# Two barriers of a decode kernel: the first weight load issued ahead of the entry barrier, the closing barrier moved in among the last matmuls

## The chip, the cores and the metric

The profile lists the instructions of five engines. In the kernel before, TensorE (PE in the profile, PEld for its weight loads; 12682 of each) multiplies matrices, VectorE (DVE, 574), ScalarE (ACT, 454) and GpSimd (POOL, 27) do the other arithmetic, and SyncE (SP) issues the large loads, 280.50 MB on one queue, which 16 DMA engines carry out. The engines wait for each other by semaphores: in the program an instruction or a DMA raises a number (`then_inc`), and another engine waits until it has reached a value (`wait_ge`). A drain is an instruction that each engine has in front of a barrier. In the closing barrier of the kernel before, TensorE's ended 0.06 us behind its last matmul, VectorE's 0.05 us behind the copy, and SyncE's 0.48 us behind the issue of the store and 0.53 us ahead of the store's landing. A barrier is a place that no engine passes before all have reached it: in that one the last drain ended at 655.66 us and the first engine was released at 655.81. The granted clock is the share of its full clock that the profile shows for TensorE, 0.771 on average in the kernel before.

The kernel runs on one core of one Trainium2 chip. The metric is device time in microseconds (us), the lower the better. The kernel before took 657.67 us (median of 3 runs, 657.65 to 657.86), and 657.71 us over the 6 runs of the first comparison.

Two lengths occur in this text. The *time* is the metric. The *span* is what the profile draws: from the first recorded instruction to the last. The time is longer than the span by about 1.5 us. The result of each run lists its time to 0.01 us and its span to 0.1 us. Where "time minus span" is given below it is the mean over all runs of a kernel.

## The reference, cut to what matters

```python
def reference(A_x, A_k_cache, A_v_cache, A_wq, A_wo, B_x, B_w1, B_b1, B_w2, B_b2):
    # A: one decode token; 32 query heads, 8 KV heads, 65536 keys of 128, D = 512
    #    q = xn @ wq ; p = softmax(q k^T / sqrt(128)) ; o = p v ; result o @ wo
    # B: gelu(xn @ w1 + b1) @ w2 + b2, hidden size 1792
    x = A_x
    xn = _layernorm(x, axis=-1)
    return x + _A_ref(xn, A_k_cache, A_v_cache, A_wq, A_wo) + _B_ref(xn, B_w1, B_b1, B_w2, B_b2)
```

One token is decoded, so every weight and every cached key and value is read once. K and V are 134 MB each, wq and wo 4.2 MB each, w1 and w2 1.8 MB each. The output is 1 KB.

## The kernel before: the parts that matter

All large loads go out on SyncE's queue in a fixed order. Each wait is a semaphore wait that the program inserts from the recorded dependences.

```python
    dma_small()        # ACT queue: x row (1 KB), b2 (1 KB), b1 (3.5 KB)
    dma_wq()           # SP queue: 4 MB, no wait in front of it
    dma_w12()          # SP queue: w1, w2, 1.8 MB each
    issue_chunks()     # SP queue: K halves of 4 MB, V of 8 MB, as their slots come free;
                       # ... last of all wo in pieces (4, 2 and 1 KV heads, then 3+1 query heads)
```

The end, after the rolled loop over 16 pairs of K/V chunks:

```python
    for i, (g0, n) in enumerate(WP):                 # wo pieces 0, 1, 2
        for r in range(g0 * HPG, (g0 + n) * HPG):
            for kt in range(KT):
                fin_mm(kt, oX_bf[:, r:r + 1], wo_sb[:, r, ...], ["oX", f"wo{i}"], ...)
    for h in range(HPG):                             # the last piece: the last KV head's rows
        for kt in range(KT):
            fin_mm(kt, oT_all[:, ...], wl_sb[:, h, ...], ["oL", ...], ...)
    # copy PSUM -> fin_bf on DVE, store fin_bf -> out on SP
    # ...
    with nc.Block() as block:          # entering: jump of every engine into its own code
        # ... one body per engine: _emit(...) of everything recorded above
    # leaving the block: a barrier of all five engines
    sp.wait_ge(ev_out.sem, ev_out.val) # SyncE alone waits for the store
```

The barriers are not written out in the kernel. An entry barrier stands at the head of the program, behind the setting of some constants on GpSimd. A closing barrier stands where the block ends. In both, every engine drains and signals GpSimd, and GpSimd then releases all of them: in the entry barrier of the trace the last drain, GpSimd's, ends at 0.50 us, GpSimd's two semaphore instructions stand at 0.54 and 0.62, and the others are released at 0.66 to 0.67; in the closing barrier of the trace the last drain ends at 655.66 us, GpSimd's two semaphore instructions stand at 655.69 and 655.77, and the others are released at 655.81 to 655.82.

## Time and profile before

| | before |
|---|---|
| time, median of 3 | 657.67 us |
| span of the profiled execution | 656.2 us |
| moved | 280.65 MB, mean 428 GB/s |
| TensorE busy | 536.5 us (82%) |

The page's slice table cuts the span into 40 equal slices. A digit is the busy share in tenths, 9 meaning 90% or more. The DMA section names the queues.

```profile
span 656.2 us, 27968 instructions
...
PE   2387799978789697878969788896978879787897
...
DMA  8999999999999999999999999999999999999997
...
q1 hardware_dynamic: 8616, 280.50, 99.3%
```

The DMA engines are full from the second slice to the second last, while TensorE has gaps. The packet records in the trace say it more sharply: between 2.07 us and 651.63 us no stretch of over 150 ns has fewer than 12 of the 16 DMA engines at work. So the span is a first wait, then a stream that the DMA engines set and not the compute engines, then a tail.

The head, from the timeline (start, duration, engine, line, operation; `SPq` and `ACTq` are the queue instructions of SyncE and ScalarE; in brackets the idle time before and what ended it):

```profile
0.74 0.53 ACTq L454 DMA_DIRECT2D rows_bf<-in_A_x_dram  x1
...
0.75 0.39 SPq L463 DMA_DIRECT2D kv<-in_A_wq_dram  x1
...
1.20 0.41 SPq L467 DMA_DIRECT2D kv<-in_B_w_dram  x1
...
2.95 0.40 DVE L499 CAST x_row<-rows_bf 1x512 f32<-1x512 bf16 x1
...
8.75 0.16 DVE L521 CAST xnT_bf<-pA 128x4 bf16<-128x4 f32 x1 [0.38 <-PE pA L518]
...
13.30 3.15 PE L525 MATMUL pss<-kv,xnT_bf 128*1 128x512 bf16 x28 [4.59 <-DMA kv<-in_A_wq_dram]
```

SyncE drains at 0.00 us and is released at 0.66. The first packet of wq moves at 1.77 us, by the packet records. Layernorm is done at 8.9 us and TensorE then waits 4.59 us for wq.

The tail, from the timeline, and the instructions of the closing barrier (durations in ns, then the start in us):

```profile
652.62 0.39 PE L805 MATMUL pss<-kv,oX_bf 128*1 128x128 bf16 x16 [0.22 <-DMA kv<-in_A_wo_dram]
...
653.72 0.46 PE L805 MATMUL pss<-kv,oT_all 128*1 128x128 bf16 x16 [0.70 <-DMA kv<-in_A_wo_dram]
654.23 0.29 DVE L820 CAST fin_bf<-pss 97x128 bf16<-97x128 f32 x1 [5.01 <-PE pss L805]
654.55 0.63 SPq L824 DMA_DIRECT2D out_dram<-fin_bf  x1
```

```profile
L828 POOLq EVENT_SEMAPHORE  x2: 17/17/17, 655.7 to 655.8; - x2
...
L828 SPq DRAIN  x1: 417/417/417, 655.2 to 655.2; - x1
...
L828 PEldq EVENT_SEMAPHORE  x1: 51/51/51, 655.8 to 655.8; - x1
```

The queue's own waits of SyncE (us in total, times, longest):

```profile
SPq L850 <- DMA out_dram<-fin_bf: 0.4, 1, 0.4
SPq L828 <- PEq L828: 0.2, 1, 0.2
```

SyncE issues the store, drains for 0.42 us, passes the barrier at 655.8 us, and then still waits 0.4 us for the store.

### The profile page before, as it was taken

Reading aid. Unit: us, or ns where it says so; the run is one execution under the profiler, and the core shown is the slowest. Engines: PE = TensorE matmul, PEld = TensorE weight load, DVE = VectorE, ACT = ScalarE, POOL = GpSimd, SP = SyncE. Lnnn points to the kernel's source line nnn. Section 1 sums busy time; section 2 is a strip of 40 time slices with the busy share of each in tenths; the row PEclk is TensorE's granted clock in tenths of the full one; section 3 lists DMA queues with packets and bytes.
Section 4 is the critical chain, followed back from the end, with each engine's and each line's share of the span. In section 5 each row is a group of like instructions: output and inputs, shape, how many; then the busy total and the mean of one; then the engine's idle time right before and its main releaser. Section 6 shows DMA issues by size and latency. Waiting matters only on the chain.

```text
span 656.2 us, 27968 instructions
## 1 busy us (share of the span) xinstructions
PE 536.5 (82%) x12682; PEld 509.5 (78%) x12682; DVE 275.3 (42%) x574; ACT 244.9 (37%) x454; POOL 2.9 (0%) x27
## 2 busy tenths in 40 slices
PE   2387799978789697878969788896978879787897
PEld 0186798978688697868959787895978879786886
DVE  3244162725435162453516345261534516154353
ACT  0134162624425153352505335160443516244251
POOL 0000000000000000000000000000000000000000
PEclk9788596968869597786958778595876959688696
DMA  8999999999999999999999999999999999999997
GB/s 367 431 450 424 426 431 431 437 425 465 397 437 443 423 439 425 437 429 439 437 419 447 417 441 421 429 463 399 451 417 457 425 419 437 425 465 397 434 429 307
DMA packets 8774, 280.65 MB, mean 428 GB/s; under 512 B 1082, under 2 KB 1596, under 8 KB 1724
## 3 DMA queue, kind: packets, MB, share of 16 engines
q1 hardware_dynamic: 8616, 280.50, 99.3%
q8 instruction: 8, 0.13, 0.1%
q10 hardware_dynamic: 148, 0.01, 0.0%
q14 instruction: 2, 0.02, 0.0%
HBM read 280.50 MB, written 0.00 MB: 427 GB/s over the span
## 4 chain that ended last, share of the span: by engine, by line
DMA 64%; PE 34%; issue 2%; DVE 0%; SPq 0%
DMA kv<-in_A_k_cache_dram 61%; PE pst L590 27%; PE pss L610 4%; DMA kv<-in_A_wo_dram 3%; PE pO L681 2%; PE pA L637 0%; PE pA L648 0%; DVE pmax L618 0%; PE pA L697 0%; DVE gmax L639 0%; PE pss L805 0%; DVE diag L641 0%; SPq L470 0%; SPq L467 0%; SPq L463 0%
## 5 line engine op out<-in xcount | busy, mean ns | idle before, releaser
L600 ACT ACTIVATE kt_ring<-pst 128x1024 bf16<-128x1024 bf16 x192 | 195.6, 1027 | 310.7 <-PE pst L590 309.2
L590 PE MATMUL pst<-ident_bf,kv 128*128 128x128 bf16 x4096 | 282.0, 235 | 35.3 <-DMA kv<-in_A_k_cache_dram 35.2
L590 PEld LDWEIGHTS pst<-ident_bf,kv 128*128 128x128 bf16 x4096 | 263.7, 106 | 43.6 <-DMA kv<-in_A_k_cache_dram 36.8
L598 DVE COPY kt_ring<-pst 128x1024 bf16<-128x1024 bf16 x320 | 210.5, 687 | 120.4 <-PE pst L590 118.1
L681 PE MATMUL pO<-P_bf,kv 128*128 128x4 bf16 x4096 | 115.1, 166 | 38.2 <-DMA kv<-in_A_v_cache_dram 34.2
L681 PEld LDWEIGHTS pO<-P_bf,kv 128*128 128x128 bf16 x4096 | 113.6, 104 | 39.6 <-DMA kv<-in_A_v_cache_dram 35.3
L610 PE MATMUL pss<-q_cur,kt_ring 128*128 128x4 bf16 x4096 | 111.9, 164 | 4.3 <-issue 4.3
L610 PEld LDWEIGHTS pss<-q_cur,kt_ring 128*128 128x128 bf16 x4096 | 109.3, 96 | 4.5 <-issue 4.5
L659 ACT ACTIVATE P_bf<-pss,negm 128x128 bf16<-128x128 f32 x128 | 50.8, 547 | 68.0 <-DVE negm L651 68.0
L690 DVE COPY o_all<-pO 128x4 f32 (+1 forms) x32 | 5.2, 162 | 121.4 <-PE pO L681 120.6
L618 DVE TENSOR_REDUCE pmax<-pss 128x4 f32<-128x512 f32 x32 | 22.1, 691 | 68.2 <-PE pss L610 68.2
L659 ACT ACTIVATION_READ_ACCUMULATOR P_bf<-pss,negm 128x1 f32 x128 | 35.3, 276 | 0.0
L648 PEld LDWEIGHTS pA<-diag,ones_f 4*128 4x128 f32 x64 | 12.6, 244 | 17.9 <-DVE diag L641 16.3
L637 PE MATMUL pA<-ident_f,pmax 128*4 128x128 f32 x64 | 14.0, 307 | 12.5 <-DVE pmax L618 12.5
L648 PE MATMUL pA<-diag,ones_f 4*128 4x4 f32 x64 | 15.4, 309 | 10.0 <-DVE diag L641 10.0
L637 PEld LDWEIGHTS pA<-ident_f,pmax 128*4 128x4 f32 x64 | 2.9, 84 | 15.7 <-DVE pmax L618 14.0
L639 DVE TENSOR_REDUCE gmax<-pA 4x1 f32<-4x128 f32 x32 | 8.8, 274 | 9.2 <-PE pA L637 9.2
L673 DVE COPY sums_all<-sums 128x8 f32 (+1 forms) x16 | 2.7, 171 | 23.4 <-ACT P_bf L659 23.4
L697 PE MATMUL pA<-sums_all,ones_f 128*128 128x128 f32 x32 | 12.4, 491 | 0.0
L651 DVE TENSOR_SCALAR negm<-pA 128x4 f32<-128x4 f32 x32 | 5.1, 160 | 10.8 <-PE pA L648 10.8
L697 PEld LDWEIGHTS pA<-sums_all,ones_f 128*128 128x128 f32 x32 | 8.0, 312 | 0.0
L641 DVE TENSOR_SCALAR diag<-ident_f,gmax 4x4 f32<-4x4 f32 x32 | 6.9, 217 | 1.1
(78 smaller groups left out, 48.3 us busy)
## 6 DMA issues: line engine op xcount, KB each, us to landing
kv<-in_A_k_cache_dram SPq DMA_DIRECT2D x32, 4096.0 KB, 27.6
kv<-in_A_v_cache_dram SPq DMA_DIRECT2D x4, 4096.0 KB, 24.4
kv<-in_A_wq_dram SPq DMA_DIRECT2D x1, 4096.0 KB, 12.4
kv<-in_B_w_dram SPq DMA_DIRECT2D x2, 1792.0 KB, 18.2
kv<-in_A_wo_dram SPq DMA_DIRECT2D x1, 2048.0 KB, 24.2
kv<-in_A_wo_dram SPq DMA_DIRECT2D x1, 1024.0 KB, 26.4
kv<-in_A_wo_dram SPq DMA_DIRECT2D x1, 512.0 KB, 27.2
kv<-in_A_wo_dram SPq DMA_DIRECT2D x1, 384.0 KB, 17.6
```

The costliest lines, as they stand in the source:

```text
L590: lambda tb=tb, at=at, b=b, tt=s * TPB + t: pe.transpose(pst[tb][:, at * 128:(at + 1) * 128], slot[b][:, tt, :], ident_bf[:, :]),
L598: e, fn = DVE, lambda tb=tb, dst=dst: dve.tensor_copy(out=dst, in_=pst[tb][:, :])
L600: e, fn = ACT, lambda tb=tb, dst=dst: act.activation(out=dst, in_=pst[tb][:, :], func=ACTF.Copy)
L610: lambda k=k, kb=kb, at=at, t=t: pe.matmul(pss[k][:, at:at + HPG], lhsT=kt_ring[:, kb * BCOL + t * 128:kb * BCOL + (t + 1) * 128], rhs=q_c ...
L618: lambda k=k: dve.tensor_reduce(out=pmax[:, :], in_=pss[k][:, 0:CW].rearrange("p (t j) -> p j t", j=HPG), axis=AX.X, op=ALU.max),
L637: sch.op(PE, lambda: pe.matmul(pA[0:HPG, PA_ST:PA_ST + 128], lhsT=pmax[:, 0:HPG], rhs=ident_f[:, :], start=True, stop=True), reads=["pmax" ...
L639: sch.op(DVE, lambda: dve.tensor_reduce(out=gmax4[:, :], in_=pA[0:HPG, PA_ST:PA_ST + 128], axis=AX.X, op=ALU.max), reads=["pA"], writes=[" ...
L641: sch.op(DVE, lambda: dve.tensor_scalar(out=diag4[:, :], in0=ident_f[0:HPG, 0:HPG], scalar1=gmax4[0:HPG, 0:1], scalar2=None, op0=ALU.mult) ...
L648: sch.op(PE, lambda: pe.matmul(pA[:, PA_SB:PA_SB + HPG], lhsT=ones_f[0:HPG, 0:128], rhs=diag4[0:HPG, 0:HPG], start=True, stop=True), reads ...
L659: lambda k=k, at=at, j=j, src=src: act.activation(out=P_v[k][:, :, j], in_=src[:, :, j], func=ACTF.Exp, bias=negm[:, at:at + 1], scale=1.0 ...
L681: lambda k=k, t=t: pe.matmul(pO[:, 0:HPG], lhsT=vslot[:, k * TPD + t, :], rhs=P_v[k][:, t, :], start=t == 0, stop=t == TPD - 1),
L697: sch.op(PE, lambda: pe.matmul(pA[:, PA_SUM:PA_SUM + NC], lhsT=ones_f[:, :], rhs=sums_all[:, :], start=True, stop=True), reads=["ones_f", ...
```

## The change

The intent is to take both barriers off the ends. The load of wq waits for nothing, so it can be issued before SyncE reaches the entry barrier. The closing barrier can stand where TensorE would wait for the next wo piece anyway (0.54 us in the kernel before), and the last matmuls, the copy and the store then follow it.

```diff
+    rest = {}
     for i, (g0, n) in enumerate(WP):
+        if i == 1:
+            rest.update((e, len(e.ops)) for e in (PE, DVE, SP))
         for r in range(g0 * HPG, (g0 + n) * HPG):
@@
+    first, SP.ops[0] = SP.ops[0], ([], None, None)
+    assert not first[0]
+    head = nc.cur_bb.bb.instructions
+    n = len(head)
+    first[1]().then_inc(*first[2])
+    at = next(k for k, ins in enumerate(head) if ins.engine == mybir.EngineType.SP
+              and type(ins).__name__ == "InstDrain")
+    moved = [head.pop() for _ in range(len(head) - n)]
+    for ins in moved:
+        head.insert(at, ins)
@@
-            _emit(e, SP.ops)
+            _emit(e, SP.ops[:rest[SP]])
@@  (DVE and PE likewise)
+    for e, obj in ((PE, pe), (DVE, dve), (SP, sp)):
+        _emit(obj, e.ops[rest[e]:])
     sp.wait_ge(ev_out.sem, ev_out.val)
```

More of the change, by code (lines that the diff above doesn't have):

```diff
@@ L843, in _ @@
         def _(e):
-            _emit_rolled(e, DVE.ops, [m[0] for m in marks2], pair)
+            _emit_rolled(e, DVE.ops[:rest[DVE]], [m[0] for m in marks2], pair)
         @block.tensor
         def _(e):
-            _emit_rolled(e, PE.ops, marks)
+            _emit_rolled(e, PE.ops[:rest[PE]], marks)
+    for e, obj in ((PE, pe), (DVE, dve), (SP, sp)):
+        _emit(obj, e.ops[rest[e]:])
     sp.wait_ge(ev_out.sem, ev_out.val)
```

## The prediction

> What bounds the kernel now. The slice table shows the 16 DMA engines busy 0.9 or more in every slice but the first (8) and the last (7), at about 430 GB/s; the DMA section shows 280.5 MB on SyncE's queue. The transfer records are stricter: from 2.07 us to 651.63 us no stretch over 150 ns has fewer than 12 of the 16 engines at work. A 4 MB K transfer lands a median 27.6 us after its issue, though 4 MB at 430 GB/s takes under 10 us, so another transfer is always queued. TensorE is busy 82% but waits for K and V landings (35.2 and 34.2 us in the waits view). The span is therefore: time to the first byte, about 650 us of stream, and a tail after the last wo byte. This edit can change only the first and last.
>
> Head. In the timeline SyncE's drain stands at 0.00 us, the entry barrier releases it at 0.66, its wq issue runs 0.75 to 1.13, first data moves at 1.77. Issued ahead of the drain, wq should start at 0.0 to 0.1 and its first byte move at 1.0 to 1.1. Cost: SyncE reaches the barrier after its 0.39 us issue and a drain that may take as long as the one behind the store (0.42 us), so the barrier releases near 0.9 to 1.1. That delays the x row, the memsets and the layernorm by 0.2 to 0.4 us, which is free: layernorm was done at 8.9 us and TensorE then waited for wq until 13.3. The w1 issue stays near 1.0 to 1.2 us, while wq feeds the engines for about 10 us. The whole gain, 0.65 to 0.75 us, lies on the critical path, and as the queue never runs dry it should reach the end undiminished.
>
> Tail. The last wo piece lets TensorE go at 653.72; matmuls 0.49, copy 0.29, store issue 654.55 to 655.18, SyncE's drain 0.42, barrier released at 655.81, then still 0.4 us of wait until the store lands at 656.19. The closing barrier is already hidden behind the store's flight; moving it saves nothing.
> The moved barrier costs TensorE a drain (0.29 us) and a release (about 0.2 us) after the first wo piece, which ended at 650.83; the second started at 651.37. It may now start up to 0.2 us late, but pieces two and three wait 0.5 to 0.7 us for data afterwards, which absorbs it. Net tail: 0.
>
> Sum: 657.67 - 0.7 = 656.95; 0.1% faster, so "same". Range 656.6 to 657.4.
>
> What the profile would show. Right: first wq data near 1.05 us; stream length unchanged within 0.2 us; later landings 0.7 us earlier; the stretch from last matmuls to end still about 2.5 us and ended by the store's landing. Wrong: a slow first issue; a starved queue after wq; TensorE idle after the moved barrier for a reason other than data.
>
> What would make it wrong. [...] this trace has four waits of about 2 us in TensorE's first loop pass with no recorded cause. If the jump behind the barrier caused one, the gain becomes a loss of about 1 us. Or the measured time includes work after the last instruction that idle engines can start sooner: then up to 0.4 us more gain. Or the stream's rate differs by 0.1%, which hides everything.

## The result, and the profile after

The changed kernel took 656.82 us (median of 6 runs, 656.69 to 656.90) against 657.71 us for the kernel before. The ratio is 0.9986, with a 95% interval from 0.9973 to 0.9999. By the 2% rule that is "same". A ratio is the mean time of one kernel's fast runs over that of the other's in the same rounds, so it is not quite the ratio of the two medians.

The head after the change:

```profile
0.00 0.39 SPq L463 DMA_DIRECT2D kv<-in_A_wq_dram  x1
...
0.79 0.52 ACTq L454 DMA_DIRECT2D rows_bf<-in_A_x_dram  x1
...
0.80 0.33 SPq L467 DMA_DIRECT2D kv<-in_B_w_dram  x1
...
7.21 0.41 DVE L499 CAST x_row<-rows_bf 1x512 f32<-1x512 bf16 x1 [4.13 <-DMA rows_bf<-in_A_x_dram]
...
13.03 0.16 DVE L521 CAST xnT_bf<-pA 128x4 bf16<-128x4 f32 x1 [0.39 <-PE pA L518]
...
13.25 3.58 PE L525 MATMUL pss<-kv,xnT_bf 128*1 128x512 bf16 x32 [0.25 <-DVE xnT_bf L521]
```

The issue of wq now stands at 0.00 us and its first packet moves at 1.02 us. The barrier released SyncE at 0.71 us, only 0.05 us later than before: the drain behind this issue took 0.12 us and ended at 0.57, and in the kernel before the barrier had waited for GpSimd anyway, whose drain behind its constants ended at 0.50. But look at the x row. It is issued 0.05 us later and is used 4.3 us later, at 7.21. Its 1 KB packet moved at 5.53 us instead of 1.66 us: it now finds the DMA engines already full of wq (from 1.35 us on, 12 or more of the 16 at work). Its landing was told at 7.12 us instead of 2.00. The delay is more than one recorded packet of wq: those (32 KB each) took 1.2 to 2.2 us, and the x row moved 3.9 us later than before. How the DMA engines share their time between the two queues no run here shows. wq landed at 12.31 us instead of 13.17, but TensorE's first projection starts at 13.25 us instead of 13.30: it now waits for the layernorm, not for wq, and is no earlier than before.

The tail after the change:

```profile
650.55 1.02 PE L805 MATMUL pss<-kv,oX_bf 128*1 128x128 bf16 x32 [0.33 <-PEq L842]
...
651.76 0.60 PE L805 MATMUL pss<-kv,oX_bf 128*1 128x128 bf16 x16 [0.18 <-DMA kv<-in_A_wo_dram]
...
652.85 0.60 PE L805 MATMUL pss<-kv,oT_all 128*1 128x128 bf16 x16 [0.50 <-DMA kv<-in_A_wo_dram]
653.50 0.29 DVE L823 CAST fin_bf<-pss 97x128 bf16<-97x128 f32 x1 [4.78 <-PE pss L805]
653.82 0.64 SPq L827 DMA_DIRECT2D out_dram<-fin_bf  x1
```

```profile
L842 POOLq EVENT_SEMAPHORE  x2: 17/17/17, 650.3 to 650.4; - x2
...
L842 PEldq DRAIN  x1: 893/893/893, 649.4 to 649.4; - x1
...
L842 PEldq EVENT_SEMAPHORE  x1: 51/51/51, 650.4 to 650.4; - x1
```

```profile
SPq L866 <- DMA out_dram<-fin_bf: 1.0, 1, 1.0
```

```profile
SPq L866 <- DMA out_dram<-fin_bf: 1.0, 1, 1.0
```

The barrier releases TensorE at 650.44 us, and the second wo piece landed at that very moment, 650.44. The next two pieces again wait for data. SyncE waits 1.0 us for the store instead of 0.4, so the 0.6 us that the barrier took there became waiting: nothing was won inside the span.

Here is the whole difference of the two profiled executions, from the instruction, packet and landing records (us):

| stretch | before | after | difference |
|---|---|---|---|
| start to the first packet of wq | 1.77 | 1.02 | -0.75 |
| first packet to the end of the last wo packet | 651.72 | 651.61 | -0.11 |
| to the start of the last piece | 0.23 | 0.22 | -0.01 |
| last piece, up to the copy | 0.51 | 0.65 | +0.14 |
| copy to the end of the span | 1.99 | 1.99 | 0.00 |
| span | 656.22 | 655.49 | -0.73 |
| time minus span | 1.58 | 1.32 | -0.26 |
| time | 657.80 | 656.81 | -0.99 |

The time minus span is that of two single executions here; the means over all runs, below, differ by 0.17 us.

The +0.14 us goes with the granted clock. The two windows below (length, busy us and count of TensorE, granted clock, DMA share, GB/s) are of the same microsecond, before and then after:

```profile
653.00:654.00 1.00, 0.29 (x20) 1.00 0.05 17
```

```profile
653.00:654.00 1.00, 0.45 (x16) 0.50 0.00 0
```

The clock records alternate between 1.00 and 0.50 from 17.5 us to the end in the kernel before, in stretches of up to 20.5 us. Which of the two the last piece meets differs between the profiled executions (one of each program) and is not an effect of the change: in three of the later experiments that contain the whole change (e5, e6 and e7) the clock stands at 1.00 there and this stretch takes 0.51 us, in e1, e8 and e10 it stands at 0.50 and takes 0.65 us. For example e7:

```profile
653.00:654.00 1.00, 0.38 (x16) 1.00 0.00 0
```

Two things were left to explain. Is the head alone responsible for the shorter span? And where does the gain outside the span come from?

### The profile page after: what moved, and what is told of

Same layout as the page of the kernel before. It is cut to its first block, busy times and chain, and to the rows that moved or that the text cites. A ratio compares the mean times of both kernels' runs of the same rounds, so it can differ in the third digit from the quotient of the medians.

```text
span 655.5 us, 27968 instructions
## 1 busy us (share of the span) xinstructions
PE 536.8 (82%) x12682; PEld 509.6 (78%) x12682; DVE 275.8 (42%) x574; ACT 245.0 (37%) x454; POOL 2.9 (0%) x27
## 4 chain that ended last, share of the span: by engine, by line
DMA 63%; PE 34%; issue 2%; DVE 0%; SPq 0%
DMA kv<-in_A_k_cache_dram 61%; PE pst L590 27%; PE pss L610 4%; DMA kv<-in_A_wo_dram 3%; PE pO L681 2%; PE pA L637 0%; PE pA L648 0%; DVE pmax L618 0%; PE pA L697 0%; PE pss L805 0%; DVE gmax L639 0%; DVE diag L641 0%; SPq L470 0%; SPq L467 0%; DVE fin_bf L823 0%
```

## The experiments

The theory going in: the head earns the first byte's 0.75 us and the moved barrier earns nothing inside the span. For the 0.2 us outside the span there were two candidates. Theory A says it is noise, or tied to the shape of the code. Theory B says the time includes end work of each engine after its last recorded instruction, and idle engines start it sooner once the barrier is gone from the end. The rival is that the barrier was on the path inside the span.

All times below are means of the runs of one job (e1 to e4, e5 to e8, e9 to e11 and e12 each on one chip, with the kernel before beside them). All outputs are right.

| run | edit | time | against before of the job | span | time minus span |
|---|---|---|---|---|---|
| before (four jobs) | | 657.61 to 657.73 | | 656.14 to 656.23 | 1.46 to 1.51 |
| e1 | the whole change | 656.75 | -0.98 | 655.42 | 1.33 |
| e2 | head only | 656.98 | -0.74 | 655.48 | 1.50 |
| e3 | tail only | 657.52 | -0.20 | 656.16 | 1.36 |
| e4 | before, second closing barrier | 657.96 | +0.24 | 656.14 | 1.82 |
| e5 | change, GpSimd waits for the store | 657.40 | -0.32 | 655.52 | 1.87 |
| e6 | change, ScalarE waits | 657.03 | -0.69 | 655.52 | 1.50 |
| e7 | change, TensorE waits | 657.16 | -0.56 | 655.52 | 1.63 |
| e8 | change, VectorE waits | 657.05 | -0.66 | 655.58 | 1.48 |
| e9 | before, four more entry barriers | 659.27 | +1.55 | 657.52 | 1.74 |
| e10 | change, five loads ahead | 656.75 | -0.97 | 655.38 | 1.37 |
| e11 | change, barrier in front of the copy | 657.11 | -0.61 | 655.67 | 1.44 |
| e12 | tail only, four more entry barriers | 659.14 | +1.53 | 657.58 | 1.56 |

The intervals of the ratios are about 0.13 to 0.17% of the time wide on each side, near 1 us, so a single ratio proves little here: e3's -0.20 us has the interval 0.9984 to 1.0011. What carries the argument are the spans, the time minus span, and the records of the trace, which repeat much better (before: 1.50, 1.49, 1.51 and 1.46 us in four jobs).

### e1 to e3: the whole change and its halves

> The changed kernel again, as the yardstick for the parts on the same chip. Theory (the head alone pays inside the span): 0.85 to 0.95 us under before, span 0.7 us shorter, first wq data near 1.02 us instead of 1.77, the closing stretch ended by the store's landing. If the last pieces ran at granted clock 0.50 only by chance of phase, this profile may show 1.00 there, and then a span near 655.35.

e2 keeps the head part of the diff alone, e3 the tail part alone:

```diff
 # e2, against before
+    first, SP.ops[0] = SP.ops[0], ([], None, None)
+    ...                                     # the moved issue, as in the change
 # e3, against the change
-    first, SP.ops[0] = SP.ops[0], ([], None, None)
-    ...
```

> Only the first issue is moved. Theory A (closing barrier hidden behind the store, and nothing outside the span counts): all of the gain, 0.7 to 0.9 us, as e1_both within 0.1 us. Theory B (the time also holds work after the last instruction that the other engines start sooner once the barrier is gone from the end): the span shrinks by about 0.7 us but the time gains only about 0.7, some 0.2 us less than e1_both, and time minus span stays near 1.55 us as in before.

> Only the barrier is moved. Theory A: no change in span or time (within 0.15 us; the last piece may take 0.49 or 0.62 us by the granted clock). Theory B: span unchanged, time 0.2 us lower, time minus span near 1.33 us as in the changed kernel. Rival (the barrier was on the path): span 0.3 to 0.6 us shorter.

The head alone shortens the span by 0.74 us (656.22 to 655.48) and the time by the same 0.74 us. Its first packet moves at 1.02 us. The tail alone leaves the span where it was (656.22 and 656.16; its runs scatter from 655.9 to 656.5) and lowers the time minus span from 1.50 to 1.36 us. The halves add up: 0.74 + 0.20 is 0.94, against 0.98 for the whole. So the span's gain is the head's, and the gain outside the span is the moved barrier's. Noise, the one half of theory A, and the rival (an effect inside the span) both fall. Theory B fits, but these three runs do not exclude that the shape of the code sets the time outside the span; e4 to e8 take that up. e1's hope for a full clock at the end did not come true: the clock stood at 0.50 again.

### e4: a second barrier at the end

```diff
+    nc.all_engine_barrier()
     sp.wait_ge(ev_out.sem, ev_out.val)
```

> The kernel before with one more barrier right behind the closing one. The closing barrier releases at 655.82 us and the store lands at 656.19, so 0.37 us of slack. Theory A: a second barrier of about 0.2 to 0.3 us fits into the slack, span and time unchanged within 0.1 us. Theory B: span unchanged, time 0.2 to 0.3 us higher, because the other engines end that much later. Rival (barrier on the path): both 0.2 to 0.3 us higher.

The second barrier released the engines at 656.15 us instead of 655.82, and SyncE's wait for the store still ended the span: 656.2 us in the profile, a mean of 656.14. The time minus span went up from 1.50 to 1.82 us, by 0.32 us, as much as the release came later (0.33 us). So a cost can be entirely hidden within the span and still be paid in the time.

### e5 to e8: which engine?

Each of these is the changed kernel with one more line, for one engine each:

```diff
     sp.wait_ge(ev_out.sem, ev_out.val)
+    pool.wait_ge(ev_out.sem, ev_out.val)      # e5; act in e6, pe in e7, dve in e8
```

> The changed kernel, with GpSimd also waiting for the store at the very end. So far time minus span is 1.50 us where all engines are held by the closing barrier until 0.4 us before the end (before, head only), 1.82 with a second barrier, and 1.33 to 1.36 where the others were released 4 us earlier. Theory B: some engine has about 0.55 us more end work than SyncE. If it is GpSimd: span unchanged, time minus span about 1.9 us, time about 657.3. If not: 1.33 and 656.75. Theory A (outside-span time is noise or tied to the code's shape): no difference between the four engines.

> The same with ScalarE waiting for the store. If ScalarE has the longer end work: time minus span about 1.9 us, time about 657.3; if not 1.33 and 656.75.

> The same with TensorE waiting for the store. If TensorE has the longer end work: time minus span about 1.9 us, time about 657.3; if not 1.33 and 656.75.

> The same with VectorE waiting for the store. If VectorE has the longer end work: time minus span about 1.9 us, time about 657.3; if not 1.33 and 656.75.

The four engines now end at the same moment as SyncE, one at a time. The time minus span is 1.87 us for GpSimd, 1.63 for TensorE, 1.50 for ScalarE and 1.48 for VectorE, against 1.33 when SyncE ends alone. It is GpSimd, as one of the two outcomes had it; that the other three cost 0.15 to 0.3 us too had not been expected. These four programs differ in one engine's name alone, so the shape of the code does not explain their differences; what one more waiting instruction costs by itself none of them tells. Now the kernel before can be estimated: its GpSimd ended at 655.78 us, and 1.87 us more gives 657.65, while SyncE ended at 656.22 and 1.33 us more gives 657.55. By this estimate GpSimd, released by the closing barrier, was the engine that finished last in the kernel before, by about 0.1 us, a little less than the 0.14 to 0.18 us that the moved barrier gained. The same sum fits e4: GpSimd's last instruction ended at 656.12 us there, and 1.87 more gives 657.99, against a mean time of 657.96. In that time the traces of the kernel before and of the changed kernel list no instruction, but their semaphore records go on: 245 semaphores are updated once each between 0.31 and 0.98 us behind the span in the kernel before, and 234 between 0.26 and 0.85 us in the changed kernel. Which engine does it, and what else is done in that time, no run here shows.

### e9: the first byte delayed on purpose

```diff
+    for _ in range(4):
+        nc.all_engine_barrier()
     with nc.Block() as block:
```

> The kernel before with four more entry barriers, to dose the delay of the first byte. One barrier took 0.33 us in e4, so wq is issued at about 2.1 us and its first data move at about 3.1 us instead of 1.77. Theory (the head counts one to one, as the stream never runs dry): span and time both 1.3 us longer, about 659.0. Rival (the first loop passes or the layernorm set the pace, the stream catches up): clearly less than 1.3 us.

The issue of wq stood at 2.09 us and its first packet moved at 3.11 us instead of 1.77, 1.34 us later. The span grew by 1.31 us (656.21 to 657.52). The head counts one to one, in both directions. The time grew by more, 1.55 us, because the time minus span also grew, from 1.51 to 1.74 us. The account did not explain that, and e12 takes it up.

### e10: more loads ahead of the barrier

```diff
-    first[1]().then_inc(*first[2])
+    for _, fn, pub in SP.ops[:5]:
+        fn().then_inc(*pub)
+    SP.ops[:5] = [([], None, None)] * 5
```

> The changed kernel with all five first loads (wq, w1, w2, two K) issued ahead of the entry barrier, not wq alone. The entry barrier then releases near 2.5 us and the x row comes about 1.8 us later. Theory (only the first byte counts): first data at 1.02 us as before, time as the changed kernel within 0.15 us, 656.75; layernorm ends near 10.5 us, still before wq lands at 12.3. Rival (more issues ahead pay too): a further 0.2 us or more.

Nothing more was gained: a mean of 656.75 us, as e1. Only the first byte counts, because the queue behind it is never empty: by the packet records of e10 no stretch of over 150 ns has fewer than 12 DMA engines at work between 1.24 and 651.95 us, and in the changed kernel none between 1.35 and 651.52 us. One number of the expectation missed: layernorm was not done near 10.5 us. The x row was issued at 2.83 us, and the timeline of e10 shows what followed:

```profile
8.30 0.41 DVE L499 CAST x_row<-rows_bf 1x512 f32<-1x512 bf16 x1 [3.17 <-DMA rows_bf<-in_A_x_dram]
...
14.13 0.16 DVE L521 CAST xnT_bf<-pA 128x4 bf16<-128x4 f32 x1 [0.39 <-PE pA L518]
...
14.35 3.58 PE L525 MATMUL pss<-kv,xnT_bf 128*1 128x512 bf16 x32 [0.25 <-DVE xnT_bf L521]
```

The projection started 1.1 us later than in the changed kernel, 1.95 us after wq had landed at 12.40, and even that cost nothing. The first load that waits for this early work, a V load, was issued at 26.76 us in e10 instead of 25.00, while K loads issued before it landed until 41.56 us.

### e11: the barrier where nothing hides it

```diff
-        if i == 1:
-            rest.update((e, len(e.ops)) for e in (PE, DVE, SP))
@@
     NR = 32 * (KT - 1) + 1
+    rest.update((e, len(e.ops)) for e in (PE, DVE, SP))      # barrier behind the last piece
```

> The changed kernel with the barrier moved on, from the second wo piece to behind the last piece, in front of the copy and the store: there nothing hides it. Theory: TensorE's drain (0.29 to 0.43 us) and the release (about 0.15 us) stand between the last matmul and the copy, so the span grows by 0.3 to 0.5 us against the changed kernel, time minus span falls or stays at 1.33, time 657.05 to 657.25. Rival (a barrier is free wherever it stands as long as it is not last): 656.75.

In the profile of e11 the copy waits for the barrier:

```profile
652.77 0.59 PE L805 MATMUL pss<-kv,oT_all 128*1 128x128 bf16 x16 [0.46 <-DMA kv<-in_A_wo_dram]
653.70 0.29 DVE L822 CAST fin_bf<-pss 97x128 bf16<-97x128 f32 x1 [4.91 <-PEq L841]
```

From the start of the last piece to the copy it took 0.92 us, against 0.65 in the changed kernel at the same clock of 0.50: 0.28 us for the drain and the release, just under the expected 0.3 to 0.5. The author's estimate is that most of the drain overlaps the matmuls there, as in the changed kernel, where TensorE's drain took 0.89 us and ended 0.05 us behind the last matmul. The mean time was 0.36 us above e10, which ran on the same chip. Of this the span has 0.30 us. The time minus span was expected to fall or to stay at 1.33 us and was 1.44, against 1.37 in e10; no run explains that part. The barrier is not free wherever it stands; at the second wo piece it is free because TensorE has to wait for data there.

### e12: the unexplained part of e9

```diff
 # against e3
+    for _ in range(4):
+        nc.all_engine_barrier()
     with nc.Block() as block:
```

> The kernel with only the closing barrier moved (e3), and the four extra entry barriers of e9. In e9 the span grew by the 1.3 us that the first byte was late, but time minus span also grew, from 1.51 to 1.74 us, which the account so far does not explain. If the extra 0.24 us is end work of GpSimd behind the closing barrier, the moved barrier hides it: span 1.3 us over e3 (657.5), time minus span back at 1.33 to 1.40, time near 658.85. If it is additive (something in front of the span, or end work that nothing hides): time minus span about 1.6, time near 659.1.

Again the first byte came 1.35 us later (3.11 against 1.76 in e3) and the span was 1.42 us longer than e3's (another chip; the befores' spans are 0.08 us apart). The time minus span was 1.56 us, against 1.36 in e3, so the extra 0.2 us is still there: it is additive, and not GpSimd's end work behind the closing barrier. Where it sits, ahead of the span or after it, no run tells. The moved barrier is worth something here too: 1.74 us in e9 and 1.56 here, on two chips whose befores had 1.51 and 1.46. One consequence must be drawn: the four barriers added to the program cost about 0.2 us outside the span, 0.05 us each if they share it equally, for a reason that stays open, so some of e4's 0.32 us may be of that kind. e2, e3 and e5 add no barrier and are not touched by it.

No experiment points to a version faster than the changed kernel. e10 equals it. The floor of 1.33 us outside the span is SyncE's own, or of whatever follows it, and nothing tried here lowered it.

## Why the prediction was right, and where it was off

The prediction was 656.95 us with a range of 656.6 to 657.4, and "same". Measured were 656.82 us and "same". Point by point:

- **What bounds the kernel: right.** "As the queue never runs dry it should reach the end undiminished": e2 gained 0.74 us in span and time, e9 lost 1.31 us of span for 1.34 us of first byte, and e10 gained nothing from more loads ahead.
- **The size of the head: right.** Predicted were 0.65 to 0.75 us and a first packet near 1.05 us; measured were 0.74 us (e2) and 1.02 us.
- **The barrier's delay at the head: over-estimated, without effect.** A drain of up to 0.42 us was allowed for and a release at 0.9 to 1.1 us; the drain took 0.12 us and the release came at 0.71.
- **The x row: wrong by a factor of ten or more, without effect.** The prediction said that the layernorm is delayed "by 0.2 to 0.4 us". It was delayed by 4.3 us (8.75 to 13.03 for its last step), because only the later issue had been costed (0.05 us as measured), and not the time from the issue to the packet, 4.7 us with wq ahead of it against 0.9 before. That is more than the wait for wq could cover: the projection started 0.9 us after wq had landed (13.25 and 12.31). It cost nothing all the same, because the next load that depends on this work is issued while others are still queued (at 25.00 us, with K loads landing until 41.53); in e10 the projection started a further 1.1 us later and the time stayed.
- **The tail inside the span: right.** "Net tail: 0": copy to end took 1.99 us in both, e3's span did not change, and the second wo piece started as its data landed. No wait without a recorded cause was seen behind the moved barrier: 0.11 us from the release to the matmul.
- **The tail as a whole: the step that failed.** "The closing barrier is already hidden behind the store's flight; moving it saves nothing." It was hidden in the span and not in the time. Moving it saves 0.14 to 0.18 us of time minus span (e3 against before, e1 against e2). The prediction had named this case, "up to 0.4 us more gain", as a way to be wrong and had put nothing for it in the sum. With 0.74 for the head and 0.17 for the tail the sum is 656.80 us, taken from 657.71.
- **Chance.** The profiled execution shows the last piece 0.14 us slower by the granted clock and the stream 0.11 us shorter. The first comes and goes between programs; for the second, the same stretch takes 651.39 to 651.73 us over all fourteen traces, with or without the moved issue.

## What to carry to other kernels

Where the DMA engines stream without a gap, as here (12 or more of 16 at work from 2.07 to 651.63 us), what an edit like this one can cut is the time to the first byte and the tail behind the last byte, and what was won or lost at the head came through nearly whole (0.74 us of 0.75, 1.31 of 1.34); issue the first load ahead of everything, but look at which small loads now stand behind it (here the x row, used 4.3 us later). A cost that the span hides may still be paid (0.14 to 0.18 us here, 0.32 in e4): let engines that have nothing more to do end early, and do not hold all of them at a barrier in the last microsecond. Put a barrier that must exist where the busiest engine is waiting for data anyway (nothing in the span at the second wo piece, 0.28 us in front of the copy).

## What the steps cost here

- The time minus span was 1.87 us with GpSimd ending last, 1.63 with TensorE, 1.50 with ScalarE, 1.48 with VectorE and 1.33 with SyncE alone (e5, e7, e6, e8 and e1).
- The 1 KB store in the kernel before took 1.64 us from issue to landing, of which 0.63 was the issue and 1.23 had passed when the first packet moved; from the end of the last packet to the landing it was 0.34 us.
- The 1 KB x row moved 4.7 us after its issue (0.79 to 5.53 us) and landed 6.3 us after it when wq was 0.8 us ahead of it, and it moved 0.9 us after its issue (0.74 to 1.66) and landed 1.3 us after it when both were issued together.
- A barrier took 0.33 us from release to release when all engines are idle (e4; four took 1.34 us in e9), and 0.28 us between TensorE's last matmuls and VectorE's copy in e11. Four added ones also cost about 0.2 us outside the span (e9 and e12), cause open.
